# Router logits of the last five token blocks: weights stationary, four partial sums, one joining matmul

## The chip, the cores and the metric

The kernel runs on one core of a Trainium2 chip. The metric is the device time of one execution in microseconds. Engines are named as in the profile: PE is TensorE's matmul, PEld its weight load, DVE VectorE, ACT ScalarE, POOL GpSimd, SP the engine that issues most transfers.

## The reference

Attention with pooled queries gives x (1152 tokens x 512); a gated feed-forward layer maps x to x; then a router sends each token to the two best of eight experts. The part that matters here is the router's product of the tokens with two 512 x 8 matrices:

```
logits = x @ w_gate
noise_scale = np.log1p(np.exp(x @ w_noise))
noisy_logits = logits + noise_scale * noise
top2 = np.argpartition(-noisy_logits, 2, axis=1)[:, :2]
...
top2_w = np.exp(top2_l)
top2_w /= top2_w.sum(-1, keepdims=True) + 1e-09
...
        h = np.maximum(x[mask] @ w1[e], 0.0)
        out[mask] += top2_w[mask, k, None] * (h @ w2[e])
```

## The kernel before

The 1152 tokens are nine blocks of 128. The whole program is one list of instructions written out by hand: each engine executes its own in the order in which the Python code issues them, and a tile framework adds the waits between engines. The feed-forward phase consists of 48 units (`unit`, L524) of 24 matmuls. After 6, 12, 18 and 24 matmuls a unit calls `slot`, which issues whatever has been put at that position with `at(4 * unit + slot, ...)`. So `T_L[4] = 187` means behind the last matmul, and behind the activations, of unit 46. `T_L[5] = 191` is the same place in unit 47, the last one.

For each block the router does three things. `r_trans` (L653) transposes the block's 128 x 512 outputs X2 with four matmuls (L656), and ScalarE copies them to `xrt` (L658). The product with the router's weights `wgn` (512 x 32, of which 16 columns are the two matrices) goes to the PSUM bank `LG`. `r_top` (L690) then makes the noisy logits and the two best experts from all blocks of one half: three activations (L695 to L697), then a chain of small VectorE steps from L700 to L728.

The product exists in two forms. `r_logits` (L660) takes the transposed block as the stationary operand: four products of 128 x 16, which accumulate over the four quarters of 512. In the trace these are eight matmuls and eight weight loads of 128 columns. `r_part` (L667) takes the weights as the stationary operand, 32 columns at a time, with each quarter in its own 32-row strip of the bank; ScalarE copies the 128 x 128 result (L675), and `r_join` (L677) adds the four strips with one matmul against `jn`. Blocks 0 to 3 use `r_part` and `r_join`, blocks 4 to 8 `r_logits`.

Around blocks 4 to 8 this is the order. Blocks 4 and 5 are in the slots of units 46 and 47. Then `x_trans0` (L989) transposes two gathered blocks of the first expert's tokens (`xg`, gathered by GpSimd at L976); between its two halves stand a dummy Exp on ScalarE (L1353), which loads the activation table, and block 6. The last two feed-forward outputs (`xout`, L550, matmuls L557, added by VectorE at L562) follow. After them the expert phase begins. `w_hi` (a cast on ScalarE, L106) and `w_lo` (a subtraction on VectorE, L1014) split the expert's weights, `up` multiplies (L1081), `up_evac` evacuates (L1085 on ScalarE, L1086 on VectorE), `down` multiplies (L1108). `run(gB, n)` issues the next n steps of the router's chain for blocks 4 to 8 (`r_top`, then `r_assign`, L731) between the products of the first expert. Further on the chain yields the tables of tokens per expert, the indices for the next gathers and the numbers of the experts whose weights are loaded next.

Of the kernel before, what the change touches and what calls it, by code (L numbers as in the profile page):

```python
# [9 lines left out]
F32 = mybir.dt.float32  # L10
# [11 lines left out]
def fused_kernel(ctx, tc, q, k, v, w_gate, w_val, w_out, rms_g,  # L22
                 r_gate, r_noise, noise, e_w1, e_w2, out, dbg=None):
    nc = tc.nc
    P = 128
# [8 lines left out]
    DT = H * D // P  # L34
    SCALE = 0.5 / float(D) ** 0.5

    pe, dve, act, pool, sp = nc.tensor, nc.vector, nc.scalar, nc.gpsimd, nc.sync
# [26 lines left out]
    xp = lx.enter_context(tc.tile_pool(name="xp", bufs=1))  # L64
# [130 lines left out]
    xT, rs, es, ET, AV, accp, smS = {}, {}, {}, {}, {}, {}, {}  # L195
# [229 lines left out]
    for p in range(NPB):  # L425
        F = [[] for _ in range(2 * NST)]

        def at(i, f, *a):
            F[i].append((f, a))
# [120 lines left out]
    def xout(f, hf, t):  # L550
        c0 = t * P - HALF[hf][0]
        pt = ps.tile([P, 512], F32, name="po", tag="po", bufs=2)
        w = [spl[f, 2][z].rearrange("p (d f) -> p d f", d=2) for z in range(2)]
        k_ = 0
        for a, b_ in ((0, 0), (0, 1), (1, 0)):
            for j in range(2):
                pe.matmul(pt, HT[f, hf][a][:, j, c0:c0 + P], w[b_][:, j, :], start=(k_ == 0), stop=(k_ == 5))  # L557
                k_ += 1
        if f == 0:
            act.copy(X2[:, t, 0:DM], pt)  # L560
        else:
            dve.tensor_tensor(X2[:, t, 0:DM], pt, X2[:, t, 0:DM], op=ALU.add)  # L562


    NE, EF = e_w1.shape[0], e_w1.shape[2]
# [9 lines left out]
    R = {}  # L575

    def rtile(nm, shape, dt=F32):
        R[nm] = rt.tile(shape, dt, name=nm)
        return R[nm]
# [66 lines left out]
    LG, PB = {}, {}  # L646
    BANK = {0: (ptab, "tab", 1), 4: (ps, "gv0", 2)}

    def bank_(spec, nm):
        pl, tg, nb = spec  # L650
        return pl.tile([P, 512], F32, name=nm, tag=tg, bufs=nb)
# [5 lines left out]
        xt = R["xt", t] = rt.tile([P, DT, P], F32, name="xrt", tag="xrt", bufs=2)  # L657
        act.copy(xt, pt.rearrange("p (d c) -> p d c", d=DT))  # L658

    def r_logits(t, t0, nt):  # L660
        if t == t0:
            LG[t0] = bank_(BANK[t0], "lg")
        o = 2 * NE * (t - t0)
        for d in range(DT):
            pe.matmul(LG[t0][:, o:o + 2 * NE], R["xt", t][:, d, :], R["wgn"][:, d, 0:2 * NE], start=(d == 0), stop=(d == DT - 1))

    def r_part(t, t0):  # L667
        if t == t0:
            LG[t0] = bank_(BANK[t0], "lg")
        o = P * (1 + t % 3)  # L670
        for d in range(DT):
            pe.matmul(LG[t0][32 * d:32 * d + 32, o:o + P], R["wgn"][:, d], R["xt", t][:, d, :], start=True, stop=True,
                      tile_position=(0, 32 * d))
        R["lp", t] = xp.tile([P, 320], F32, name="lgp", tag="smS", bufs=1)[:, 0:P]
        act.copy(R["lp", t], LG[t0][:, o:o + P])  # L675

    def r_join(t, t0):  # L677
        o = 2 * NE * (t - t0)
        pe.matmul(LG[t0][:, o:o + 2 * NE], R["lp", t], R["jn"], start=True, stop=True)
# [100 lines left out]
    def r_weights(t0, nt):  # L780
        ts_ = slice(t0, t0 + nt)
        d, e2 = R["e2"][:, 0, ts_], R["e2"][:, 1, ts_]
        w = X2[:, ts_, DM:]
        dve.tensor_scalar(d, e2, 1.0, 1e-9, op0=ALU.add, op1=ALU.add)
        yield
        dve.reciprocal(w[:, :, 0], d)
        yield
        dve.tensor_copy(w[:, :, 2:4], R["idx"][:, ts_])
        yield
        dve.tensor_tensor(w[:, :, 1], e2, w[:, :, 0], op=ALU.mult)  # L790
        yield
        for b in range(2):
            x = XD[b * SQ:b * SQ + QF].rearrange("(p c) d -> p c d", c=4)
            lo = max(t0, 5 * b)
            hi = min(t0 + nt, 5 * b + 4)
            if lo < hi:
                sp.dma_start(x[:, lo - 5 * b:hi - 5 * b, DM:], X2[:, lo:hi, DM:])
        if t0 <= 4 < t0 + nt:
            for b in range(2):
                sp.dma_start(XD[b * SQ + QF:(b + 1) * SQ, DM:], X2[b * QR:(b + 1) * QR, 4, DM:])  # L800
# [123 lines left out]
        yield  # L924

    def r_index(pl):
        tab = pl.tile([P, P], F32, name="tabs")
        act.copy(tab[0:NCOL], PB["t"][0:NCOL, 0:P])
        pi = bank_((ps, "gv1", 2), "pi")
        pe.matmul(pi[:, 0:NCU], R["tab0"][0:NCOL], R["sel"][0:NCOL], start=True, stop=False)  # L930
        pe.matmul(pi[:, 0:NCU], tab[0:NCOL], R["sel"][0:NCOL], start=False, stop=True)
        sidx, gidx = rtile("sidx", [P, NCU], I32), rtile("gidx", [P, NCU], I32)
        dve.tensor_scalar(gidx, pi[:, 0:NCU], float(BIG), float(BIG - 1), op0=ALU.add, op1=ALU.min)
        dve.tensor_scalar(sidx, pi[:, 0:NCU], float(BIG), None, op0=ALU.add)
# [284 lines left out]
    T_J = 1  # L1219
# [67 lines left out]
    def run(g, n=1000):  # L1287
        if n < 1000 and skip.get(id(g), 0):
            skip[id(g)] -= 1
            return  # L1290
        for z in itertools.islice(g, n):
            if z and n < 1000:
                skip[id(g)] = z - 1
                return
# [32 lines left out]
    for t, s_ in enumerate(T_T):  # L1327
        at(s_, r_trans, t)
    for t, s_ in enumerate(T_L):
        if t < 4:  # L1330
            at(s_, r_part, t, 0)
            at(s_ + T_J, r_join, t, 0)
        else:
            at(s_, r_logits, t, 4, 5)
    for s_, a in zip(T_S, ((0, 4), (4, 5), (5, 7))):
        at(s_, x_store, *a)
    for s_, n in enumerate(T_A[1]):
# [13 lines left out]
    gx = x_trans0()  # L1351
    next(gx)
    act.activation(R["scr"], R["scr"], AF.Exp)  # L1353
    r_logits(6, 4, 5)
    run(gx)
    xout(l_, 1, 7)
    xout(l_, 1, 8)
    x_store(7, 9)
# [2 lines left out]
    ex = experts()  # L1361
    w_hi, w_lo, wsplit, piece, x_trans = (ex[n] for n in ("w_hi", "w_lo", "wsplit", "piece", "x_trans"))
    up, up_evac, down, wload = (ex[n] for n in ("up_pair", "up_evac", "down", "wload"))
    ex["head"]()
    gW = r_weights(4, 5)
    gC = r_blocks()
    gH = r_hot(4, 5, ex["mo"], (("oha", 1), ("ohs", 3)), ())
# [11 lines left out]
    r_trans(8, (ps, "gv1", 2))  # L1379
    w_hi(0, 3)  # L1380
    w_lo(0, 3)
    up(0, 0, 1)
    r_logits(7, 4, 5)
    r_logits(8, 4, 5)
    up_evac(0, 0)
    run(gB, 1)
    up(0, 1, 0)
    w_hi(0, 4)
    ex["weight"](0)
    run(gB, 6)  # L1390
# [39 lines left out]
    down(0, 6, 1)  # L1430
    run(gC)
    r_index(ex["mo"])
    ex["weight"](1)
    ex["gather_x"](2)
# [42 lines left out]
```

## Time and profile before

| what | value |
|---|---|
| median of 3 runs | 822.1 us (821.35 to 822.17) |
| profiled execution | 823.6 us |
| its span, first to last instruction | 821.8 us |
| TensorE busy | 782.5 us, 95% |
| VectorE busy | 584.0 us, 71% |
| ScalarE busy | 416.7 us, 51% |
| mean granted TensorE clock | 0.986 |

All durations used below are those of the profiled execution. A share of busy time is a mean over attention, feed-forward and experts, three phases with different limits, so the stretch that the change touches has to be read by itself. The time beside an instruction in the timeline is its own duration; the bracket behind it says how long its engine stood idle before it, and what ended that.

### The profile page before, as it was taken

What the parts mean: (1) busy time and instruction counts of PE and PEld (TensorE: products, weight loads), DVE (VectorE), ACT (ScalarE), POOL (GpSimd) and SP (SyncE); (2) the same over time, 40 slices, a digit from 0 to 9 for tenths busy, and PEclk for the clock granted to TensorE, in tenths of its full rate; (3) what the DMA queues carried; (4) which work ended last, traced back from release to release, by engine and by line L of the source; (5) the groups of instructions that cost most, each with busy time, mean ns of one, the idle gap of its engine ahead of it and who ended that gap; (6) DMA issues with size and microseconds to landing.
All of it is one profiled execution on the core that took longest, in us unless ns stands there. A gap on an engine that the chain in (4) does not pass through costs nothing.

```text
span 821.8 us, 14014 instructions
## 1 busy us (share of the span) xinstructions
PE 782.5 (95%) x5282; PEld 678.4 (83%) x5282; DVE 584.0 (71%) x854; ACT 416.7 (51%) x823; POOL 281.4 (34%) x235
## 2 busy tenths in 40 slices
PE   5999999999999889999999999999999999999992
PEld 4877777777766789999999999879989898888991
DVE  6678678688889855765787645697676968677750
ACT  4656556566667454341333242554475656556520
POOL 8456356348415512221132100103142332423430
PEclk9999999999999989999999999999999999999996
DMA  7354232230133112331142016649987969697211
GB/s 215 85 167 124 59 102 73 59 102 15 44 117 103 52 52 73 133 102 53 57 149 55 1 52 205 217 135 361 343 307 230 340 238 346 219 354 265 82 63 34
DMA packets 72940, 118.83 MB, mean 145 GB/s; under 512 B 7582, under 2 KB 37278, under 8 KB 72864
## 3 DMA queue, kind: packets, MB, share of 16 engines
q1 hardware_dynamic: 67504, 101.55, 38.7%
q0 software_dynamic: 5360, 16.31, 5.8%
q8 instruction: 43, 0.70, 0.4%
q14 instruction: 33, 0.27, 0.1%
HBM read 103.66 MB, written 10.77 MB: 139 GB/s over the span
## 4 chain that ended last, share of the span: by engine, by line
PE 78%; DVE 7%; DMA 5%; ACT 4%; issue 3%; POOL 1%; POOLq 0%; ACTq 0%; DVEq 0%
PE gv L536 14%; PE py L1108 12%; PE ph L1081 11%; PE av L229 9%; PE po L557 8%; PE st L202 5%; PE s L188 5%; PE st L203 4%; DMA xg<-XD,gidx 4%; PE tt L135 2%; ACT et L204 1%; PE ph L1096 1%; PE xt L981 1%; DVE Ql L193 1%; DVE wz L1014 1%
## 5 line engine op out<-in xcount | busy, mean ns | idle before, releaser
L536 PE MATMUL gv<-XN,ws 128*128 128x256 f32 (+1 forms) x1152 | 169.0, 300 | 4.3 <-ACT sl L544 3.7
L536 PEld LDWEIGHTS gv<-XN,ws 128*128 128x128 f32 x1152 | 160.7, 192 | 10.3 <-ACT sl L544 3.9
L1014 DVE TENSOR_TENSOR wz<-raw,wz 128x1024 fp32r<-128x1024 f32 x112 | 134.1, 1221 | 12.8 <-ACT wz L106 12.0
L193 DVE TENSOR_REDUCE Ql<-s 128x1 fp32r<-128x1152 f32 x72 | 97.3, 1355 | 53.3 <-PE s L188 32.9
L1108 PE MATMUL py<-wz,hTT 128*128 128x512 f32 x552 | 134.1, 395 | 0.0
L204 ACT ACTIVATE et<-st 128x288 f32<-128x288 f32 x288 | 103.4, 417 | 40.6 <-PE st L203 38.2
L106 ACT CAST wz<-raw 128x1024 fp32r<-128x1024 f32 x112 | 113.5, 1046 | 8.0 <-PE py L1108 8.0
L1108 PEld LDWEIGHTS py<-wz,hTT 128*128 128x128 f32 x552 | 100.7, 188 | 20.2 <-DVE hTT L986 0.9
L401 POOL TENSOR_TENSOR ws<-wm,ws 128x1024 fp32r<-128x1024 f32 x18 | 43.7, 2427 | 154.2 <-ACT ws L400 104.8
L202 PE MATMUL st<-QH,KT 128*128 128x288 f32 x288 | 92.0, 335 | 2.4 <-ACT et L204 1.0
L1081 PEld LDWEIGHTS ph<-xgT,wz 128*128 128x128 f32 x768 | 92.5, 189 | 0.7
L1081 PE MATMUL ph<-xgT,wz 128*128 128x256 f32 x768 | 92.8, 281 | 0.0
L557 PE MATMUL po<-ws,hT 128*128 128x512 f32 x324 | 83.0, 395 | 0.1
L203 PE MATMUL st<-QlT,KT 128*128 128x288 f32 x288 | 81.6, 297 | 0.0
L229 PE MATMUL av<-et,v 128*64 128x288 f32 x576 | 77.4, 412 | 0.5 <-ACT xT L234 0.5
L202 PEld LDWEIGHTS st<-QH,KT 128*128 128x128 f32 x288 | 54.6, 190 | 21.9 <-issue 12.3
L557 PEld LDWEIGHTS po<-ws,hT 128*128 128x128 f32 x324 | 58.4, 188 | 10.6 <-ACT hT L546 0.4
L546 ACT CAST hT<-sl 128x256 fp32r<-128x256 f32 (+1 forms) x48 | 20.8, 433 | 91.4 <-DVE sl L545 91.4
L1142 POOL DMA_INDIRECT out_dram<-yo,sidx x23 | 33.2, 1445 | 97.0 <-DVE yo L1141 47.6
L229 PEld LDWEIGHTS av<-et,v 128*64 128x64 f32 x576 | 38.3, 137 | 27.7 <-issue 3.9
L217 DVE TENSOR_TENSOR es<-es,et 128x576 f32<-128x576 f32 x64 | 59.7, 933 | 1.5
L203 PEld LDWEIGHTS st<-QlT,KT 128*128 128x128 f32 x288 | 55.0, 191 | 0.1
(250 smaller groups left out, 1107.2 us busy)
## 6 DMA issues: line engine op xcount, KB each, us to landing
raw<-in_moe_w_dram SPq DMA_DIRECT2D x112, 512.0 KB, 7.6
wraw<-in_moe_w_gate_dram SPq DMA_DIRECT2D x6, 1024.0 KB, 5.2
wraw<-in_moe_w_val_dram SPq DMA_DIRECT2D x6, 1024.0 KB, 5.2
wraw<-in_moe_w_out_dram SPq DMA_DIRECT2D x6, 1024.0 KB, 5.1
kraw<-in_k_dram SPq DMA_DIRECT2D x16, 288.0 KB, 3.5
v<-in_v_dram SPq DMA_DIRECT2D x8, 576.0 KB, 3.8
KT<-KT SPq DMA_DIRECT2D x16, 288.0 KB, 3.1
Qraw<-in_q_dram SPq DMA_DIRECT2D x16, 256.0 KB, 4.2
```

The source lines that it names most:

```text
L106: act.copy(o, i)
L193: dve.tensor_reduce(Ql[p % 3][h][:, c, D:D + 1], t[:, :, 0:384], axis=AX.XY, op=ALU.max, negate=True)
L202: pe.matmul(t[:, 0:NG], KT[p, h][:, cs], QhT[p, h][:, n0:n0 + NG], start=True, stop=False)
L203: pe.matmul(t[:, 0:NG], KT2[h][p % NKT[h]][:, cs], QlT[p, h][:, n0:n0 + NG], start=False, stop=True)
L204: act.activation(et[:, h, :], t[:, 0:NG], AF.Exp, scale=SCALE)
L217: eng.tensor_tensor(acc, acc, e, op=ALU.add)
L229: pe.matmul(av[h * D:(h + 1) * D, 0:NG], V[p][:, h, c, :], ET[p, g, c][:, h, :], start=(c == 0), stop=(c == KC - 1))
L536: pe.matmul(t[:, 0:n], w[a][:, d, j * P:(j + 1) * P], XN[hf][b_][:, d, cs], start=(k_ == 0), stop=(k_ == 11))
L557: pe.matmul(pt, HT[f, hf][a][:, j, c0:c0 + P], w[b_][:, j, :], start=(k_ == 0), stop=(k_ == 5))
L1014: eng.tensor_tensor(lo, RAW[u % 2][i], hi.bitcast(F32), op=ALU.subtract)
L1081: pe.matmul(o, w[a][:, d, j * P:j * P + P], XT[u][c][:, d], start=z + d == 0, stop=z == 2 and d == 3)
L1108: pe.matmul(PL[u, "y", k], x[c][:, f0 + d, k * P:k * P + P], w[a][:, d], start=i == 4 and z + d == 0, stop=i == 7 and z == 2 and d == 1)
```

## The change

`r_logits` is removed. Blocks 4 to 8 use `r_part` and `r_join` as blocks 0 to 3 do. The partial sums of blocks 4, 5 and 6 go through the one buffer that blocks 0 to 3 use; those of blocks 7 and 8 use a buffer of the expert phase, shared with the tile `tabs`. The joins of blocks 5 to 8 are put by hand behind other work of TensorE.

```diff
--- before.py
+++ after.py
@@ -657,13 +657,6 @@
         xt = R["xt", t] = rt.tile([P, DT, P], F32, name="xrt", tag="xrt", bufs=2)
         act.copy(xt, pt.rearrange("p (d c) -> p d c", d=DT))
 
-    def r_logits(t, t0, nt):
-        if t == t0:
-            LG[t0] = bank_(BANK[t0], "lg")
-        o = 2 * NE * (t - t0)
-        for d in range(DT):
-            pe.matmul(LG[t0][:, o:o + 2 * NE], R["xt", t][:, d, :], R["wgn"][:, d, 0:2 * NE], start=(d == 0), stop=(d == DT - 1))
-
     def r_part(t, t0):
         if t == t0:
             LG[t0] = bank_(BANK[t0], "lg")
@@ -671,7 +664,10 @@
         for d in range(DT):
             pe.matmul(LG[t0][32 * d:32 * d + 32, o:o + P], R["wgn"][:, d], R["xt", t][:, d, :], start=True, stop=True,
                       tile_position=(0, 32 * d))
-        R["lp", t] = xp.tile([P, 320], F32, name="lgp", tag="smS", bufs=1)[:, 0:P]
+        if t > 6:
+            R["lp", t] = R["mo"].tile([P, P], F32, name="lgq", tag="tabs", bufs=1)
+        else:
+            R["lp", t] = xp.tile([P, 320], F32, name="lgp", tag="smS", bufs=1)[:, 0:P]
         act.copy(R["lp", t], LG[t0][:, o:o + P])
 
     def r_join(t, t0):
@@ -924,7 +920,7 @@
         yield
 
     def r_index(pl):
-        tab = pl.tile([P, P], F32, name="tabs")
+        tab = pl.tile([P, P], F32, name="tabs", tag="tabs", bufs=1)
         act.copy(tab[0:NCOL], PB["t"][0:NCOL, 0:P])
         pi = bank_((ps, "gv1", 2), "pi")
         pe.matmul(pi[:, 0:NCU], R["tab0"][0:NCOL], R["sel"][0:NCOL], start=True, stop=False)
@@ -1327,11 +1323,10 @@
     for t, s_ in enumerate(T_T):
         at(s_, r_trans, t)
     for t, s_ in enumerate(T_L):
-        if t < 4:
-            at(s_, r_part, t, 0)
-            at(s_ + T_J, r_join, t, 0)
-        else:
-            at(s_, r_logits, t, 4, 5)
+        t0 = 4 * (t // 4)
+        at(s_, r_part, t, t0)
+        if t < 5:
+            at(s_ + T_J, r_join, t, t0)
     for s_, a in zip(T_S, ((0, 4), (4, 5), (5, 7))):
         at(s_, x_store, *a)
     for s_, n in enumerate(T_A[1]):
@@ -1351,8 +1346,10 @@
     gx = x_trans0()
     next(gx)
     act.activation(R["scr"], R["scr"], AF.Exp)
-    r_logits(6, 4, 5)
+    r_join(5, 4)
+    r_part(6, 4)
     run(gx)
+    r_join(6, 4)
     xout(l_, 1, 7)
     xout(l_, 1, 8)
     x_store(7, 9)
@@ -1362,6 +1359,7 @@
     w_hi, w_lo, wsplit, piece, x_trans = (ex[n] for n in ("w_hi", "w_lo", "wsplit", "piece", "x_trans"))
     up, up_evac, down, wload = (ex[n] for n in ("up_pair", "up_evac", "down", "wload"))
     ex["head"]()
+    R["mo"] = ex["mo"]
     gW = r_weights(4, 5)
     gC = r_blocks()
     gH = r_hot(4, 5, ex["mo"], (("oha", 1), ("ohs", 3)), ())
@@ -1379,12 +1377,14 @@
     r_trans(8, (ps, "gv1", 2))
     w_hi(0, 3)
     w_lo(0, 3)
+    r_part(7, 4)
     up(0, 0, 1)
-    r_logits(7, 4, 5)
-    r_logits(8, 4, 5)
+    r_join(7, 4)
+    r_part(8, 4)
     up_evac(0, 0)
+    up(0, 1, 0)
+    r_join(8, 4)
     run(gB, 1)
-    up(0, 1, 0)
     w_hi(0, 4)
     ex["weight"](0)
     run(gB, 6)
```

## Rows read from the trace of the kernel before

**Rows 1.** The page's busy times: busy us (share of the span) xinstructions of each engine.
```profile
PE 782.5 (95%) x5282; PEld 678.4 (83%) x5282; DVE 584.0 (71%) x854; ACT 416.7 (51%) x823; POOL 281.4 (34%) x235
```

**Rows 2.** Chain that ended last, 500 to 600 us: start us, us, what.
```profile
515.83 3.52 DMA xg<-XD,gidx
...
555.22 11.52 PE ph L1081 x96
```

**Rows 3.** Timeline of block 0: start us, us, engine, line, operation, xcount [idle before].
```profile
468.25 0.16 PEld L672 LDWEIGHTS lg<-xrt,wgn 128*32 128x32 f32 x8
...
468.61 0.77 PEld L536 LDWEIGHTS gv<-XN,ws 128*128 128x128 f32 x6 [0.20 <-issue]
...
468.74 0.27 ACT L675 COPY lgp<-lg 128x128 f32<-128x128 f32 x1 [0.51 <-PE lg L672]
...
469.31 0.31 PEld L679 LDWEIGHTS lg<-jn,lgp 128*128 128x128 f32 x2
...
469.53 1.00 PEld L536 LDWEIGHTS gv<-XN,ws 128*128 128x128 f32 x6
```

**Rows 4.** Timeline, TensorE's weight loads around blocks 5 to 8.
```profile
519.45 0.42 PEld L981 LDWEIGHTS xt<-ident,xg 128*128 128x128 f32 x4 [0.70 <-ACT hT L546]
...
520.84 0.42 PEld L981 LDWEIGHTS xt<-ident,xg 128*128 128x128 f32 x4
...
521.23 2.60 PEld L557 LDWEIGHTS po<-ws,hT 128*128 128x128 f32 x12
...
527.07 1.50 PEld L1081 LDWEIGHTS ph<-xt,wz 128*128 128x128 f32 x12
...
528.50 1.87 PEld L665 LDWEIGHTS lg<-wgn,xrt 128*128 128x128 f32 x16
...
530.30 7.18 PEld L1081 LDWEIGHTS ph<-xt,wz 128*128 128x128 f32 x60
```

**Rows 5.** Timeline, ScalarE around blocks 6 to 8.
```profile
520.21 0.58 ACT L984 CAST xt<-xt 128x512 fp32r<-128x512 f32 x1 [1.00 <-PE xt L981]
520.81 1.28 ACT L1353 ACT_TABLE_LOAD   x1
...
522.21 0.57 ACT L984 CAST xt<-xt 128x512 fp32r<-128x512 f32 x1
...
527.44 0.59 ACT L658 COPY xrt<-xt 128x512 f32<-128x512 f32 x1 [1.33 <-PE xt L656]
527.92 1.05 ACT L106 CAST wz<-raw 128x1024 fp32r<-128x1024 f32 x1
...
530.75 0.24 ACT L697 ACTIVATE S<-S 128x40 f32<-128x40 f32 x1
```

**Rows 6.** Timeline, VectorE's steps and TensorE's wait for them.
```profile
524.29 0.69 DVE L562 TENSOR_TENSOR X<-po,X 128x512 f32<-128x512 f32 x1 [0.19 <-PE po L557]
...
531.20 0.18 DVE L700 TENSOR_SCALAR S<-S 128x40 f32<-128x40 f32 x1
...
534.09 0.69 DVE L1086 SCALAR_TENSOR_TENSOR hTT<-ph,hTT 128x512 fp32r<-128x512 f32 x1 [0.21 <-ACT hTT L1085]
...
541.17 0.18 PE L746 MATMUL pp<-mmb,lt 128*128 128x40 bf16 x1 [0.47 <-DVE mmb L744]
```

**Rows 7.** Waits of TensorE, 640 to 730 us: us in total, times, longest.
```profile
PE xt L981 <- DMA xg<-XD,gidx: 2.4, 3, 0.9
```

**Rows 8.** Busy time by stretch: us, each engine's busy us, PEclk, DMA share, GB/s.
```profile
17.20:20.70 3.50, 1.93 (x13) 1.65 (x14) 2.78 (x7) 1.27 (x4) 3.33 (x4) 1.00 0.48 116
20.77:24.18 3.41, 3.41 (x19) 3.38 (x18) 1.36 (x1) 2.56 (x7) 0.86 (x1) 0.51 0.76 220
271.80:273.80 2.00, 0.00 (x0) 0.03 (x1) 1.75 (x6) 0.00 (x0) 0.00 (x0) 1.00 0.31 57
286.34:290.07 3.73, 0.00 (x1) 0.00 (x0) 2.39 (x4) 1.33 (x2) 2.49 (x3) 1.00 0.09 11
290.30:297.10 6.80, 6.19 (x29) 5.89 (x29) 4.68 (x10) 2.87 (x7) 2.07 (x1) 0.51 0.36 142
```

## The prediction

> **What bounds the kernel now.** I read the page's busy shares first, then the chain of work that ended last over the stretch that the change touches (512 to 556 us), then the timeline of that stretch engine by engine, and last the waits of TensorE after it. TensorE is busy for 95% of the span [rows 1], so the natural hope is that fewer or shorter matmuls shorten it. In the touched stretch the reader is to see something narrower: TensorE waits for rows that a gather brings in, which was issued at 515.83 and landed 3.52 us later [rows 2], and stood 0.70 us before it could transpose them [rows 4]. At 541.17 it waits 0.47 us for VectorE, which has been working through the router's top-2 chain [rows 6]. From 555.22 on the chain is matmuls of the expert units [rows 2], so whatever the first unit of that row is late, the end is late too, unless a later wait takes it up (a rival below).
>
> **The price of one block, old and new.** The two old products that stand together begin at 528.50 and the next work at 530.30, so one costs TensorE (1.80 / 2) = 0.90 us [rows 4]. The new form is in the trace for the first four blocks. The eight partial matmuls hold TensorE from 468.25 to 468.61, 0.36 us, and the row after them shows 0.20 us of that as idle "issue". The join holds it from 469.31 to 469.53, 0.22 us. Between them ScalarE copies the sums, starting 0.49 us after the partial matmuls and taking 0.27 us [rows 3]. A block thus costs 0.58 instead of 0.90, and five save 1.6 us if nothing waits. It also adds a hop TensorE, ScalarE, TensorE per block, and five copies in ScalarE's order. Each join is in TensorE's in-order stream, so all matmuls behind it wait for the copy, and the copy waits for all that stands before it in ScalarE's order.
>
> **Blocks 4 and 5.** Both lie before the transposes at 519.45 that wait for the gathered rows. Nothing that the gather depends on moves: its indices come from a product that stands before block 4. So what block 4 loses or wins (its copy comes behind the last hi-cast of its unit) and the 0.54 us that block 5 saves go into the wait of 0.70 us, which becomes about 1.1 (0.70 + 0.54, less some 0.2 for block 4). I take 0. If the gather went out earlier with them, the gain would be at most the 0.70.
>
> **Block 6.** Join 5 and partial 6 take 0.58 us where the old product took 0.90, but the transposes behind it need the second gathered block. They start at 520.84 [rows 4], 1.5 us after the first one landed; the rows do not tell whether the old product or the second landing held them. I take the landing, so no gain (at most 0.32). It matters little, because what counts is the copy of block 6. In the new order ScalarE has before it the cast of the first gathered block (520.21) and then the dummy Exp with its table load of 1.28 us at 520.81. The cast that follows starts at 522.21, which is where the copy of block 6 now stands [rows 5]. So the copy ends at 522.21 + 0.27 = 522.48, and join 6 starts at about 522.5. TensorE is done with the transposes at 521.23 and behind the join stand the two output products of L557, which began at 521.23 [rows 4]. Now they begin at 522.5 + 0.22 = 522.7: **1.5 us late**. The lateness passes on. VectorE adds the second product at 524.29 only because it waited 0.19 us for TensorE [rows 6], its first split of expert weights stands behind that, and TensorE's next products wait for the split.
>
> On the table load the row shows 1.28 us, and the Exp follows at once. The Trainium skill (ScalarE: Activation LUTs, What ACT_TABLE_LOAD costs) gives about 1283 ns for the load and 1380 ns more for a drain, some 2.66 us for a switch. By that the copy would come 1.4 us later still and my sum would grow by an estimated 1.4 us. The trace agrees with the first figure and shows no second one here, so the row decides.
>
> **Blocks 7 and 8.** I add 1.5 to the old times. Partial 7 stands where the second half of the first up-product began: 527.07 + 1.5 = 528.57, to 528.93. That half (1.43 us, 527.07 to 528.50 [rows 4]) ends at 530.36. ScalarE meanwhile has the copy of transposed block 8 (527.44 + 1.5, it waits for TensorE) and a weight cast (527.92 + 1.5 = 529.42, 1.05 us) [rows 5], so the copy of block 7 runs from 530.37 to 530.64. Join 7 waits 0.3 us and ends at 530.88; partial 8 ends at 531.24; the next up-product, pulled ahead of the router's last step, at 532.67; join 8 at 532.89. Until there TensorE has done what ended before at 530.30 + 1.43 = 531.73: it is 1.16 late, 0.3 better than after block 6, as two blocks save 0.64 and one wait costs 0.3.
>
> The router's chain is later than that, because join 8 now stands behind an up-product. Its third activation (L697) started 0.45 us after the old products' end [rows 4, 5]; now it starts at 532.89 + 0.45 = 533.34 and ends at 533.58. VectorE's first step L700 ran at 531.20, filling in right behind other work [rows 6]; now it waits until 533.6, 2.4 us late. From there to 541.17 VectorE had one gap that can take it up, 0.21 us at 534.09 [rows 6], which leaves 2.2. At 541.17 TensorE needs that chain's result (mmb): being only 1.16 late itself, its wait grows from 0.47 to 1.5 us. From there tables, indices and the second unit follow one another, all **2.2 us late**.
>
> **The sum.** 0 + 1.5 (block 6) - 0.34 (blocks 7 and 8 on TensorE) + 1.04 (what the router's chain is late beyond TensorE) = +2.2 us. The profiled execution took 823.6 us (its span is 821.8), so it would take 825.8. The profiled execution lies 1.5 above the median of the timed runs, 822.1, so against that median I predict 824.3.
>
> **Rivals.**
> *The clock falls too.* In the changed kernel TensorE would stand for some 2.6 us of the 4.1 from 518.4 to 522.5: 1.1 before the first gathered block, 0.3 before the second, 1.2 before join 6. TensorE was at half clock after 17.20 to 20.70, in which it was busy 1.93 of 3.50 us, and after the 3.73 us of idleness that ended at 290.07; after a single wait of 2.00 us ending at 273.80 it stayed at full clock [rows 8]. The new stretch is sparser than the first, but no single gap reaches the last. The two falls lasted about 3.4 and 6.8 us at 0.51, so they lost some 1.7 to 3.4 us; I take 2.1, since dense products follow. Time: 824.3 + 2.1 = 826.4.
> *Only TensorE's own lateness counts.* If VectorE has slack I do not see, for instance because the steps interleave otherwise, +1.2: 823.3.
> *A later wait takes it up (not slower).* In the later units TensorE waits three times for gathered rows, 2.4 us in all, 0.9 at most [rows 7]. If these rows land when the transfers allow and not some time after TensorE's own progress, the three waits absorb 2.2 us and the time stays at 822.1. It decides once the gathers are held by the weight loads in the DMA queues. Against it: each gather reuses a buffer that TensorE's transposes must have read first, so it should move with them.
> *The copies are hidden (faster).* If all joins find their copies done, the five blocks give up to 1.6 us: 820.5. It needs the table load to end before 521.2, and the row shows it until 522.09.
>
> **How the numbers follow.** Two new waits alone, 0.44; with the clock, 0.32; TensorE's lateness alone, 0.08; taken up later, 0.07; hidden copies, 0.09. The range runs from 822.0 (just below the case that is taken up) to 827.3 (into the clock's upper bound of 827.7); the hidden copies and the longest fall are left out. Slower than 0.2% (1.6 us, about what a measurement of this kernel can tell from no change) are the first two, 0.76. TensorE alone and the taken-up case are within it, and so is a small part of the hidden copies, as the blocks before 519.45 gain nothing: 0.17. Faster is the rest, 0.07.
>
> **What would show it.** Right: the join before L557 begins just after the Exp and the copy on ScalarE, with TensorE idle about 1.2 us before it; L700 some 2.4 us later relative to the gather's landing; TensorE's wait at L746 near 1.5 us; the first 96-matmul up-product of the second unit some 2.2 us later. Wrong: join 6 without a wait, the gather landing earlier, or the three later waits for gathered rows gone. The granted clock from 520 to 530 decides the first rival.

## The result

The changed kernel takes 826.56 us (median of 6 runs, 823.83 to 829.25); the kernel before took 822.17 beside it (6 runs, 821.35 to 822.62). The ratio is 1.0056, 95% interval 1.0035 to 1.0077: 4.4 us slower, where 2.2 were forecast. The median lies at the first rival's time (826.4), not at the likeliest case's (824.3). The interval, 2.9 to 6.3 us slower, lies wholly above the 2.2.

The profiled execution of after is its shortest run (823.83 us, span 822.0), so profile against profile (823.6 before) shows almost no loss. Two things outside the touched stretch hide it. The clock fell near 290 us in both, as [rows 8] show for before, but in this execution for a shorter time; a window of each that starts at the same time (us, each engine's busy us, PEclk, DMA share, GB/s), first after, then before:

```profile
294.00:298.00 4.00, 4.00 (x36) 4.00 (x35) 1.94 (x5) 2.91 (x9) 0.00 (x0) 1.00 0.00 0
```
```profile
294.00:298.00 4.00, 4.00 (x23) 4.00 (x23) 1.98 (x6) 2.92 (x8) 0.00 (x0) 0.60 0.00 0
```

Granted clock 1.00 and 36 matmuls against 0.60 and 23. After therefore arrives at the touched stretch 1.36 us ahead. And from the second unit to the end it needs 264.27 us, before 266.58. Both vary without this change too: in this window a second execution of before has 23 matmuls at 0.58, and a kernel that is edited only far behind it 36 at 1.00; from the second unit to the end that second execution needs 264.6. So the two are compared stage by stage. The chain of waits gives the marks (start us, us, what), before and then after:

```profile
507.23 2.75 PE po L557 x12
...
521.50 2.77 PE po L557 x12
```
```profile
505.87 2.75 PE po L557 x12
...
521.66 4.44 PE po L557 x12
...
557.73 11.52 PE ph L1077 x96
```

The first piece starts 1.36 us earlier in after, the second 0.16 later, and the 96 matmuls of the second unit 2.51 later than the 555.22 of [rows 2]. The stretch has grown by 1.36 + 2.51 = 3.87 us. Twelve output products that took 2.77 take 4.44.

The timeline of after from 518 to 526 us (start us, us, engine, line, operation, xcount, idle before and its releaser) shows why:

```profile
518.24 0.63 PE L977 MATMUL xt<-ident,xg 128*128 128x128 f32 x4 [0.98 <-DMA xg<-XD,gidx]
...
518.96 0.59 ACT L980 CAST xt<-xt 128x512 fp32r<-128x512 f32 x1 [0.74 <-issue]
519.28 0.42 PEld L977 LDWEIGHTS xt<-ident,xg 128*128 128x128 f32 x4 [0.20 <-issue]
...
519.57 1.28 ACT L1348 ACT_TABLE_LOAD   x1
...
520.86 0.20 ACT L1348 ACTIVATE scr<-scr 128x2 f32<-128x2 f32 x1
520.97 0.25 ACT L671 COPY lgp<-lg 128x128 f32<-128x128 f32 x1
...
521.27 0.40 PE L675 MATMUL lg<-jn,lgp 128*128 128x16 f32 x2 [1.33 <-ACT lgp L671]
...
521.51 4.58 PE L557 MATMUL po<-ws,hT 128*128 128x512 f32 x12
```

The same two places of TensorE in before, the gathered transposes and the output products:

```profile
519.48 0.63 PE L981 MATMUL xt<-ident,xg 128*128 128x128 f32 x4 [0.64 <-DMA xg<-XD,gidx]
...
521.25 3.00 PE L557 MATMUL po<-ws,hT 128*128 128x512 f32 x12
```

ScalarE goes from the cast to the table load, the Exp and only then to block 6's copy. Join 6 begins 0.05 us after the copy ends at 521.22, with TensorE idle 1.33 us before it, and the output products stand behind it. The windows around it, two of after and then one of before:

```profile
517.26:521.27 4.01, 1.70 (x20) 1.27 (x19) 1.52 (x3) 2.85 (x7) 1.48 (x2) 1.00 0.68 197
521.80:525.30 3.50, 3.50 (x10) 2.72 (x9) 1.32 (x2) 2.74 (x3) 0.00 (x0) 0.52 0.00 0
```
```profile
517.26:521.27 4.01, 3.37 (x32) 3.28 (x31) 1.30 (x3) 2.32 (x5) 2.85 (x3) 1.00 0.63 193
```

TensorE is busy for 1.70 of the 4.01 us before join 6 (3.37 in the same window of before), and then runs for 3.50 us at a mean granted clock of 0.52: about half speed for 3.4 us. The clock falls here; in before it stayed at 1.00 from 515 to 542 us.

Later in after, the router's second chain:

```profile
530.65 0.26 ACT L671 COPY lgq<-lg 128x128 f32<-128x128 f32 x1
...
530.97 0.30 PEld L675 LDWEIGHTS lg<-jn,lgq 128*128 128x128 f32 x2
...
533.06 0.31 PEld L675 LDWEIGHTS lg<-jn,lgq 128*128 128x128 f32 x2
...
533.74 0.24 ACT L693 ACTIVATE S<-S 128x40 f32<-128x40 f32 x1
534.01 0.18 DVE L696 TENSOR_SCALAR S<-S 128x40 f32<-128x40 f32 x1 [0.22 <-ACT S L693]
...
543.68 0.18 PE L742 MATMUL pp<-mmb,lt 128*128 128x40 bf16 x1 [1.43 <-DVE mmb L740]
```

Joins 7 and 8 wait for nothing. VectorE's first step (L696 here, L700 before) now waits for ScalarE, and TensorE waits 1.43 us for VectorE's last (L742 here, L746 before), where it waited 0.47 [rows 6].

### The profile page after: what moved, and what is told of

Read it like the earlier page. It is cut to its first block, busy times and chain, and to the rows that moved or that the text cites. A ratio compares the mean times of both kernels' runs of the same rounds, so it can differ in the third digit from the quotient of the medians.

```text
span 822.0 us, 14041 instructions
## 1 busy us (share of the span) xinstructions
PE 781.9 (95%) x5292; PEld 675.6 (82%) x5292; DVE 583.5 (71%) x854; ACT 417.6 (51%) x828; POOL 281.3 (34%) x235
## 4 chain that ended last, share of the span: by engine, by line
PE 80%; DVE 7%; ACT 4%; issue 3%; DMA 2%; POOL 1%; POOLq 0%; ACTq 0%; DVEq 0%
PE gv L536 14%; PE py L1104 13%; PE ph L1077 12%; PE av L229 9%; PE po L557 8%; PE st L202 5%; PE s L188 5%; PE st L203 4%; PE ph L1092 3%; PE tt L135 2%; PE xt L977 2%; ACT et L204 1%; DMA xg<-XD,gidx 1%; DVE Ql L193 1%; DVE wz L1010 1%
## 5 line engine op out<-in xcount | busy, mean ns | idle before, releaser
L557 PE MATMUL po<-ws,hT 128*128 128x512 f32 x324 | 84.5, 400 | 0.1
L557 PEld LDWEIGHTS po<-ws,hT 128*128 128x128 f32 x324 | 59.5, 192 | 11.1 <-ACT hT L546 0.5
```

## The experiments

Each was timed in five rounds beside the kernel before and profiled once. Four marks of each profiled execution make it comparable: A, the twelve products of L557 in the chain (507.23 above); T, the start of the first gathered transposes in the timeline (519.48); L, the start of the output products after them in the timeline (521.25); X, the 96 matmuls in the chain (555.22). The table is worked out from such rows; all times are us, and the ratio is that of the timed runs. "Half clock" is the time at about 0.5 around L.

| kernel | A to T | T to L | L to X | A to X | half clock | ratio (95%) | mean clock, timed runs |
|---|---|---|---|---|---|---|---|
| before (first profile) | 12.25 | 1.77 | 33.97 | 47.99 | none | | |
| before again | 11.85 | 1.67 | 33.93 | 47.45 | none | 1.0000 (0.9977–1.0023) | 0.9872 |
| delay in before | 12.10 | 1.67 | 36.31 | 50.08 | none | 1.0033 (1.0012–1.0054) | 0.9872 |
| old 4 to 6, new 7, 8 | 12.09 | 1.67 | 34.72 | 48.48 | none | 1.0015 (0.9997–1.0033) | 0.9872 |
| Exp later, old 7, 8 | 12.47 | 1.80 | 33.95 | 48.22 | none | 1.0018 (0.9999–1.0036) | 0.9871 |
| Exp later | 12.52 | 1.79 | 34.63 | 48.94 | none | 1.0003 (0.9987–1.0019) | 0.9871 |
| waits filled | 12.49 | 3.27 | 34.63 | 50.39 | none | 1.0024 (1.0008–1.0039) | 0.9875 |
| after | 12.37 | 3.27 | 36.22 | 51.86 | 3.4 | 1.0056 (1.0035–1.0077) | 0.983 |
| after again | 12.42 | 3.27 | 36.23 | 51.92 | 3.4 | 1.0051 (1.0034–1.0069) | 0.9845 |
| new 4 to 6, old 7, 8 | 13.48 | 3.48 | 36.27 | 53.23 | 6.8 | 1.0062 (1.0041–1.0082) | 0.9829 |

**The changed kernel once more**, without an edit, as the base of the others.

> The changed kernel once more, nothing edited. My theory: two new waits cost 2.2 us in every execution, and the clock falls to half behind the sparse stretch before join 6 in most, for about 3.4 or 6.8 us, which costs 1.7 to 3.4 us more; so times between 824 and 829 us, median near 826.5, and a profile with granted clock 0.50 somewhere between 519 and 530 us. Rival: the clock is a side matter and the spread comes from the later waits for gathered rows (2.4 us before, 0.4 in the first profile of the changed kernel); then an execution near 826.5 shows those waits near 2.4 us with the same clock as the first profile.

825.11 us (11 runs) against 821.13 (30), 1.4 below the 826.5 expected. The profiled execution took 822.63 us and shows none of the later waits for gathered rows; the rival spoke of one near 826.5, so this does not test it. The windows repeat the fall:

```profile
518.00:522.00 4.00, 1.70 (x18) 1.27 (x18) 1.41 (x3) 2.84 (x7) 0.41 (x1) 1.00 0.42 136
522.60:526.10 3.50, 3.50 (x10) 2.73 (x9) 1.26 (x2) 2.68 (x3) 0.00 (x0) 0.54 0.00 0
```

**The dummy Exp behind block 6's partial product and copy**, so that the copy need not wait for the table load:

```diff
     next(gx)
-    act.activation(R["scr"], R["scr"], AF.Exp)
     r_join(5, 4)
     r_part(6, 4)
+    act.activation(R["scr"], R["scr"], AF.Exp)
     run(gx)
```

> The dummy Exp with its table load is put behind the copy of block 6 instead of ahead of it; TensorE's and VectorE's order is unchanged. My theory: the copy is done before the second transposes end, join 6 waits less than 0.3 us, the stretch before L557 is no longer sparse enough for the clock to fall, and the time drops from 826.5 by 1.3 (wait) plus about 2 (clock) to 823 to 824. Rival, waits without the clock: by 1.3 only, to 825.2. Rival, the gather holds the stretch anyway: no change, 826.5.

821.55 us, no difference from before that can be measured; 823 to 824 was expected, from a base that came out 1.4 lower. Its timeline:

```profile
522.06 0.27 ACT L671 COPY lgp<-lg 128x128 f32<-128x128 f32 x1
...
522.36 1.28 ACT L1350 ACT_TABLE_LOAD   x1
522.38 0.30 PEld L675 LDWEIGHTS lg<-jn,lgp 128*128 128x128 f32 x2
...
522.62 3.01 PE L557 MATMUL po<-ws,hT 128*128 128x512 f32 x12
```

The copy comes ahead of the load, join 6 starts with no wait, T to L falls from 3.27 to 1.79 us, and the twelve products take 3.01 us again: full clock. The Exp and its table load, moved behind one copy on ScalarE, take away both the wait and, in this trace, the fall. It does not yet say which of the two cost what.

**The waits filled.** The wait stays, but TensorE works through it: 8 matmuls of 256 columns ahead of the first gathered transposes, 12 ahead of join 6. They are extra work whose result nothing reads.

```diff
     gx = x_trans0()
+    r_fill(8)
     next(gx)
...
     run(gx)
+    r_fill(12)
     r_join(6, 4)
```

> The changed kernel with 20 more matmuls of 256 columns, whose result nothing reads: 8 where TensorE waits for the first gathered block (about 1 us) and 12 where it waits before join 6 (about 1.4 us). Some 2.3 us more work for TensorE, and all other orders unchanged. My theory: they fit the waits, the clock stays at full rate from 518 to 530, and the time is lower than the changed kernel's by what the fall costs: 826.5 - 1.7 to 2.3 = 824.2 to 824.8. Rival, the sparse stretch is not what lowers the clock: the fall stays, and the time is 826.5 or up to 0.5 more.

823.19 us (12 runs), where 824.2 to 824.8 was expected from the same base. Timeline and windows:

```profile
516.95 1.22 PE L681 MATMUL fill<-XN,ws 128*128 128x256 f32 x8
...
519.58 1.67 PE L681 MATMUL fill<-XN,ws 128*128 128x256 f32 x12
...
521.15 0.40 PE L675 MATMUL lg<-jn,lgp 128*128 128x16 f32 x2
...
521.39 2.99 PE L557 MATMUL po<-ws,hT 128*128 128x512 f32 x12
```
```profile
516.60:521.10 4.50, 4.50 (x47) 3.89 (x46) 1.54 (x3) 3.12 (x9) 0.99 (x2) 1.00 0.55 172
521.10:525.00 3.90, 3.90 (x23) 3.31 (x22) 1.96 (x3) 3.46 (x5) 0.00 (x0) 1.00 0.00 0
```

Join 6 comes as late as in after (T to L 3.27 in both), but TensorE is busy throughout, the clock stays at 1.00 and the twelve products take 2.99 us, not 4.58. A kernel with 20 more matmuls is faster than after again by 2.3 ± 1.6 us (means of the timed runs), and in the trace A to X is 1.53 shorter. This separates the two: what is left against before is the waits (+2.06 us by the medians, 2.2 forecast; the interval is 0.7 to 3.2), what went away is the clock. One trace of each kernel shows the fall or its absence; over all timed executions the mean clock says the same: 0.983, 0.9845 and 0.9829 in the three kernels with the unfilled wait, 0.9871 to 0.9875 in the others.

**Blocks 7 and 8 as before, 4 to 6 new** (`r_logits` is back, as in the kernel before).

```diff
-    r_part(7, 4)
     up(0, 0, 1)
-    r_join(7, 4)
-    r_part(8, 4)
+    r_logits(7, 4, 5)
+    r_logits(8, 4, 5)
     up_evac(0, 0)
+    run(gB, 1)
     up(0, 1, 0)
-    r_join(8, 4)
-    run(gB, 1)
```

> Blocks 7 and 8 go back to the old product, at the old place ahead of the second up-product; blocks 4 to 6 stay in the new form. My theory: the wait for the router's chain (L742 in the changed kernel, 1.43 us) goes back to about 0.5, the second unit's first product comes 0.7 us earlier relative to the first output product of L557 than in the changed kernel, the wait before join 6 stays at 1.3 to 1.6 and so does the fall of the clock; time 826.5 - 0.7 = 825.8. Rival, the router's chain is the main cost: back to 823 or below.

826.13 us: no gain over after again (825.11, timed on the same chip), where 0.7 was expected, so this expectation missed. Waits of TensorE (us in total, times, longest), timeline and windows:

```profile
PE xt L984 <- DMA xg<-XD,gidx: 2.1, 1, 2.1
PE pp L749 <- DVE mmb L747: 0.5, 1, 0.5
```
```profile
524.43 0.61 PE L682 MATMUL lg<-jn,lgp 128*128 128x16 f32 x2 [1.33 <-ACT lgp L678]
...
524.88 5.34 PE L557 MATMUL po<-ws,hT 128*128 128x512 f32 x12
```
```profile
519.30:524.40 5.10, 1.71 (x20) 1.27 (x18) 1.48 (x3) 2.82 (x7) 0.16 (x1) 0.87 0.32 105
523.10:529.50 6.40, 5.07 (x14) 4.10 (x14) 1.72 (x3) 4.59 (x7) 0.00 (x0) 0.50 0.01 1
529.50:534.00 4.50, 3.98 (x30) 3.55 (x30) 3.74 (x4) 1.24 (x3) 0.00 (x0) 0.95 0.41 131
```

The wait for VectorE went back to 0.5 us as expected. But the gathered rows came 1 us later in this execution, TensorE had stood longer, the clock fell already during the wait before join 6, and half clock lasted 6.8 us (to just before 530) instead of 3.4. The fall took what the edit gave. The time alone could not price blocks 7 and 8 here; two later experiments do.

**Before, unedited**, once more, on the chip that also ran the three experiments after this one:

> The kernel before, nothing edited, for a second trace. The first trace of it shows 2.4 us of later waits for gathered rows and 266.6 us from the second unit's first product to the end; the five traces with the new form show 0 to 1.3 and 262.2 to 264.3. If later waits take up what the change costs (rival), this trace shows the 2.4 again, near 266. If the waits vary from execution to execution whatever the kernel, it may show 262 to 264. Time 821 to 822.

820.85 us, the base's own time. Its trace gives the table a second row of the old kernel: A to X differs by 0.5 us between two executions of the same code, all of it ahead of L. From X to the end it needs 264.6 us, with 1.5 us of later waits for gathered rows: between the two cases of the expectation, so it settles neither.

**Both waits away**: the Exp moved and 7 and 8 as before, two edits from above in one kernel.

```diff
-    act.activation(R["scr"], R["scr"], AF.Exp)
     r_join(5, 4)
     r_part(6, 4)
+    act.activation(R["scr"], R["scr"], AF.Exp)
...
-    r_part(7, 4)
     up(0, 0, 1)
-    r_join(7, 4)
-    r_part(8, 4)
+    r_logits(7, 4, 5)
+    r_logits(8, 4, 5)
     up_evac(0, 0)
+    run(gB, 1)
     up(0, 1, 0)
-    r_join(8, 4)
-    run(gB, 1)
```

> Both waits taken away: the dummy Exp behind the copy of block 6, and blocks 7 and 8 in the old form; blocks 4 to 6 in the new one. My theory: join 6 without a wait, the wait for the router's chain (mmb) back to 0.5, no fall of the clock; what stays is 0.3 us ahead of L557, so the time is that of before to 0.1%. Rival, the new form itself gains once nothing waits: 0.3 to 1 us faster than before.

821.81 against 820.78: the interval runs from 0.1 us faster to 3.0 slower, so no gain that can be measured, although three blocks use the cheaper form. In the trace A to X is 0.5 us longer than the mean of the two old ones (47.72).

**Blocks 4 to 6 as before, 7 and 8 new.**

```diff
-        at(s_, r_part, t, t0)
-        if t < 5:
+        if t < 4:
+            at(s_, r_part, t, t0)
             at(s_ + T_J, r_join, t, t0)
+        else:
+            at(s_, r_logits, t, 4, 5)
...
-    r_join(5, 4)
-    r_part(6, 4)
+    r_logits(6, 4, 5)
     run(gx)
-    r_join(6, 4)
```

> Blocks 4 to 6 in the old form (r_logits at the old places), blocks 7 and 8 in the new one. My theory: no wait before L557 and no fall of the clock, L557 to the second unit's first product 0.7 us longer than before (join 7's wait, and 1.4 us of wait at mmb in place of 0.5), so 0.7 us slower than before, 0.1%. Rival, the router's chain is the main cost: 2 us or more slower.

822.17 us, an interval that just includes no change. L to X is 34.72 us against 33.95 in the old kernel, and the wait for VectorE is the long one:

```profile
PE pp L749 <- DVE mmb L747: 1.5, 1, 1.5
```

Nearly the same, 34.63, stands in "Exp later" and "waits filled", three traces without the fall: blocks 7 and 8 cost 0.7 us by themselves.

**A delay put into before**: 20 unread matmuls of 256 columns ahead of the second unit's first product, to see whether a later wait takes a delay up.

```diff
+    b = bank_((ps, "gv1", 2), "fill")
+    for i in range(20):
+        pe.matmul(b[:, 0:256], ex["W"][1, 0][0][:, i % 2, 0:P], ex["XT"][1][0][:, i % 4], start=True, stop=True)
     fps.close()
     ex["rest"]()
```

> The kernel before with 20 matmuls of 256 columns, read by nothing, ahead of the second unit's first product: 2.35 us more for TensorE at a place behind everything that the change touches, and no wait, no change of the clock, no other order. If nothing later takes a delay up: +2.3 us. If the later waits for gathered rows take it up (rival): 0 to +0.5, and these waits are 2 us shorter than in the trace of before taken with it.

L to X grew by 2.36 us, and the kernel by 1.0 to 4.4 (ratio 1.0033). The waits that could have taken the delay up, from 560 to 790 us of this kernel:

```profile
PE xt L981 <- DMA xg<-XD,gidx: 2.4, 3, 1.3
```

They are the same 2.4 us as without the delay [rows 7]. A delay ahead of the second unit passes on to the end. The other kernels say so too: the means of their timed runs, each known to some 1.5 us, lie above before's by about what A to X has grown over the old kernel's 47.72. It is 0.7 us for 0.5 in "Exp later, old 7, 8", 0.9 for 0.8 in "old 4 to 6", 0.5 for 1.2 in "Exp later", 2.3 for 2.4 with the delay, 1.7 for 2.7 with the waits filled, 4.4 and 4.0 for 4.1 and 4.2 in after and after again, and 4.9 for 5.5 in "new 4 to 6".

One thing does not fit, and no run explains it. In the profiled executions the later waits for gathered rows come to 1.5 to 2.4 us in the three executions with the old form only, and to 0 to 1.3 in all seven with the new form somewhere; from X to the end the former need 263.7 to 266.6 us, the latter 262.2 to 264.3. The timed runs show no such gain.

## Why the prediction was right or wrong

The sign, the places and the prices of the two waits held; the likeliest case (824.3) did not, because it left the clock out, which is 1.6 of the 4.2 us that the trace shows. That the median lies within 0.2 us of the first rival's 826.4 is partly luck: that rival's 2.1 for the clock was 1.6 in the two traces, and 0.3 came from blocks 4 and 5, which were put at 0. In the terms of the sum, after and after again (A to X 51.89 on average) against the two old traces (47.72):

| term | predicted | found | from |
|---|---|---|---|
| blocks 4 and 5, up to T | 0 | +0.3 | A to T, 12.40 against 12.05 |
| block 6's copy behind the Exp | +1.5 | +1.55 | T to L, 3.27 against 1.72 |
| blocks 7 and 8 with the router's chain | +0.70 | +0.7 | L to X of three kernels without the fall |
| the clock | left to the rival, +2.1 | +1.6 | L to X, 36.22 against 34.66 |
| sum | +2.2 | +4.2 | timed medians: +4.4 and +4.0 |

**Blocks 4 and 5.** Block 4's join waits 0.29 us for its copy, about the 0.2 expected, and the wait for the gathered rows grew to 0.98 (1.1 expected). T lies 12.37 to 12.52 us behind A in five executions with the new form there and 13.48 in the sixth, 11.85 to 12.25 in the four with the old. The old ones alone spread over 0.4, so I leave open whether that belongs to the change. Two traces (after again, "Exp later, old 7, 8") name block 5's copy as what ended this wait. But in after the transposes' weights were loaded from 518.21 on while that copy ran until 518.22, and in both traces the gather landed 0.1 to 0.2 us before T, as in the others (519.35 and 519.48 in before), so it was the gather. That nothing was gained ahead of T is shown: the wait took it.

**Block 6.** The forecast placed the copy where the second cast had stood, behind the table load, and join 6 behind it with TensorE idle about 1.2 us. It was 1.33. Moving the Exp alone took the wait away, so the cause is shown. The Exp began 0.01 us after the load's end and the copy 0.11 us after the Exp's start, so nothing stood between them. The further 1380 ns that the Trainium skill gives for a switch (ScalarE: Activation LUTs, What ACT_TABLE_LOAD costs) do not show in any trace here.

**Blocks 7 and 8.** Their sum was right by a path with one error. Join 7 did not wait 0.3 us; its copy was done at 530.91, while TensorE was still in the half product ahead of it. The joins held TensorE longer instead, 0.32 (530.97 to 531.29) and 0.23, where 0.22 was taken from block 0. TensorE leaves the stretch 0.2 to 0.3 us early, near the forecast 0.34: in the three kernels without the fall join 8 ends 10.19 to 10.26 us behind L, and in before the same work 10.48. The wait at mmb was put at 1.5 and is 1.43; the run with blocks 7 and 8 alone shows it at 1.5 as well, and it falls to 0.5 and 0.6 in the two where they go back. So the loss is in VectorE's chain: a product of TensorE was made cheaper, and the chain behind it starts later. That it does so because join 8 stands behind an up-product is read from the rows; no run moved join 8 alone.

**The clock: the step that failed.** The rival had this stretch nearly right: 2.6 us of idleness expected, and 4.01 - 1.70 = 2.31 in the window; a loss of 2.1, and 1.6 in the trace. It was set second on the ground that "no single gap reaches the last". That compared the longest gap, and the longest in after is 1.33 us, well under the 2.00 us after which the clock had stayed up [rows 8]. The comparison that bore on it was the other row: 1.93 us busy of 3.50 had been followed by half clock. Here several waits close together were followed by the fall in all three traces that have them, and where the gaps were filled or the last of them was taken away the clock stayed at 1.00. Nor was "it stayed at full clock" safe to take from one execution. The same gap of 2.0 us, in code that no edit touches, was followed by half clock in two of the ten traces, "old 4 to 6" and "Exp later, old 7, 8". The windows over it, before and then the second of these:

```profile
272.00:287.00 15.00, 12.54 (x107) 11.65 (x107) 11.64 (x23) 7.63 (x17) 9.10 (x6) 1.00 0.20 72
```
```profile
272.00:287.00 15.00, 12.98 (x99) 12.21 (x99) 10.09 (x22) 6.90 (x15) 8.33 (x5) 0.89 0.21 72
```

The length of the fall varies too: 3.4 us at half clock in two traces and 6.8 in the third, where the gather came late as well. Both profiles of the unedited change are the shortest of its timed runs (823.83 and 822.63), so 1.6 may be less than what the clock costs in a typical one. The mean clocks of 0.983 and 0.9845, against about 0.987 elsewhere, come as an estimate to 4 to 7 us more at half clock in each execution.

**The rivals that fell.** Later waits did not take the delay up: the delay in before passed on, and the timed runs of all kernels follow A to X. The copies were not hidden, and with both waits taken away blocks 4 to 6 in the new form were still not faster. What blocks 4 and 5 save goes into the wait for the gather. That block 6 saves nothing (T to L is 1.80 there against 1.72) is measured; what held it was not tried.

## What to carry to other kernels

A cheaper product that adds a hop through another engine costs what stands before it in that engine's queue: list that queue instruction by instruction, and look for a table load there before moving anything into it. When a wait is added on TensorE, look at all the idle time around it and not only at its longest gap, and price the half clock that may follow as part of the wait, from more than one execution. If the wait can't be removed, unread matmuls inside it can cost less than the idleness, here by 2.3 ± 1.6 us.

## What the runs showed of the hardware

Idleness in pieces of at most 1.33 us, 2.31 of 4.01 us in all, was followed by 3.4 us at half clock in after, and the same again (2.30 of 4.00) in after again; in "Exp later", where TensorE waited 1.12 us for the gather but not at join 6, it was not. One gap of 2.0 us was followed by half clock in two of ten executions. The wait of the gathered transposes hardly follows the time at which the gather was issued: in before it was issued 8.6 us after A and in before again 6.7 us after A (515.83 and 514.15), and T stood at 12.25 and 11.85. In "new 4 to 6, old 7, 8" it was issued 6.4 us after A (514.37), and T stood at 13.48. What sets the landing was not tried.
